# Attention's result kept as f32 until the MLPs, and two buffers for P^T and P's tail

## The chip, the cores and the metric

The kernel runs on one core of a Trainium2 chip. Its time is device microseconds (us) of one execution, as a median of the runs. TensorE (PE in the profile, PEld its weight loads), VectorE (DVE), ScalarE (ACT), GpSimd (POOL) and the DMA queue of SyncE (SP) work side by side, each on its own queue in program order, and wait for each other through semaphores. Attention's and the MLPs' operands lie in SBUF; TensorE writes only to PSUM, which has eight banks.

## The reference

Attention over 4 batches, 8 heads, 576 positions and 64 values per head, with rotated q and k, and then two MLPs over all 2304 tokens of width 512:

```python
q_rot, k_rot = rotate(q), rotate(k)
scores = scale * q_rot @ k_rot.T
attn = exp(scores - max(scores)); attn = attn / (sum(attn) + 1e-9)
x = (attn @ v).transpose(0, 2, 1, 3).reshape(2304, 512)
x = (1 / (1 + exp(-(x @ moe_w_gate))) * (x @ moe_w_val)) @ moe_w_out   # 512 -> 1536 -> 512
h = x @ moe2_w_in                                                      # 512 -> 2048
out = (h * (1 / (1 + exp(-1.702 * h)))) @ moe2_w_out                   # 2048 -> 512
```

All inputs and outputs are float32. (The weights arrive as 8-byte numbers and are decoded to float32 on the core.)

## The kernel before

**Number format.** A product in the MLPs is made of three passes: each operand is kept as a high part (rounded to the format fp32r) and a low part (value minus high part), and `split_mm` (L415) adds low weights x high activations, high weights x low activations, and high x high. For the activations these parts lie in the tiles `xhl[n]`: 128 partitions, 2 parts, 4 pieces of the model width, and the columns of block n. The 2304 tokens make five blocks, four of 512 and one of 256. The whole of `xhl` lies in the pool `big`, which lives for the whole kernel, with one buffer for each block.

**Attention** goes over 16 pairs of heads (4 batches x 4), and each pair over nine units, one for each 128 queries of a head, and one for the tails of 64 queries of both heads. A unit's scores (L295, L296) go to one of two PSUM buffers `pss`; DVE takes the row maximum `nm` (L298); ACT makes the exponentials (L313) into `P` (or `Pt` for the tails, one buffer); DVE makes reciprocals `r`, POOL scales P (L331). TensorE transposes P in pieces of 128 columns against the identity (L356; the tail in L363 with 64 columns as weights, and L368) into one of three PSUM banks `pt`, which ACT (L343) or DVE (L341) copies to the SBUF tiles `PT0` (first 256 queries) and `PT1` (other 320), one buffer each. The product P V (L386, two heads side by side in 64 columns of the array each; L383 for the tails of both) is summed over five steps in the one PSUM bank `ps_x`, first with PT0, then with PT1: two pieces per pair. When a piece is done, `split` in `pv` (L403) is put on a list `later` that the next slot works off: ACT copies the piece out of PSUM as the high part into `xhl` (L407), then DVE subtracts it from PSUM into the low part (L409). A piece that crosses the edge of a block makes two such steps, so that there are 24 steps of 256 columns and 24 shorter ones. The next piece's first P V must wait for both.

**The order of attention** is written out by hand. Slot G stands for unit G % 9 of pair G / 9; tables of lags (ROPE_MUL, PT, PV) say how many slots after its pair's first one each step comes. In a slot the steps follow the list in `slot` (L587): scores first, then rotation (`rope_mul`, `rope_add`, `transpose_qk`), one step of weight decoding, the list `later`, transposes of P, loads, P V, and the exponentials. The rotated q and k of the next pairs are transposed on TensorE (L234, into a bank `pt` too), split by ACT (L243) and DVE (L244), and moved to the layouts X, Y, Z, Zs by six transfers on SP's queue (L274). All 144 units' scores are issued by slot 143; the last pair's transposes and P V follow in the drain, slots 144 to 163. After it the pools `rot` (rotation's tiles, `pss`) and `soft` (P, PT, the other PSUM banks) are closed, and the MLPs' pools are opened in the space that comes free. A tile there waits only for the tiles that it overlaps.

**The MLPs** go over chunks of 256 hidden columns (6 and 8 of them) and in each over the five blocks. `hidden` (L439) makes 48 matmuls for a block in the first MLP, 24 in the second, with four PSUM buffers `psh`; ACT and DVE make the gated product and its parts. The output product of the block before follows (`out1`, `out2`: 24 matmuls), and DVE adds it to an f32 tile `acc[n]`, which lies in the MLPs' pool. At the last chunk of the first MLP `out1` makes new high and low parts of `acc` for the second (L482 on ACT, L483 on POOL). Between blocks the next chunk's weights are loaded and decoded (L133 to L139).

Of the kernel before, what the change touches and what calls it, by code (L numbers as in the profile page):

```python
# [8 lines left out]
F32 = mybir.dt.float32  # L9
F32R = mybir.dt.float32r  # L10
U32 = mybir.dt.uint32
AF = mybir.ActivationFunctionType
# [4 lines left out]
P = 128  # L17
# [9 lines left out]
def f(ap):  # L27
    return ap.bitcast(F32)
# [3 lines left out]
def attention_then_mlps(  # L32
# [32 lines left out]
    sp = soft.enter_context(tc.tile_pool(name="soft", bufs=1))  # L65
    stage_a = soft.enter_context(tc.tile_pool(name="stage_a", bufs=1))
    ps_t = soft.enter_context(tc.tile_pool(name="ps_t", bufs=1, space=PSUM))
    rp = rot.enter_context(tc.tile_pool(name="rope", bufs=1))
    ps_s = rot.enter_context(tc.tile_pool(name="ps_s", bufs=2, space=PSUM))

    cos_sb = rp.tile([P, NCHK, D], F32, name="cos_sb")
# [2 lines left out]
    vtail = [sp.tile([P, P], F32, tag=f"vtail{n}", name=f"vtail{n}") for n in range(2)]  # L74


    xhl = {}

    def new_xhl(n):
        xhl[n] = big.tile([P, 2, KT, width[n]], F32R, tag=f"xhl{width[n]}", name=f"xhl{n}", bufs=width.count(width[n]))  # L80


    stage = [stage_a]
# [217 lines left out]
    def exps(i, u):  # L301

        j, h = divmod(u, 2)
        ps = st[i].pop(("ps", u))
        nm = st[i]["nm"][:, h, j : j + 1]
        if h == 0:
            st[i]["P"][j] = (
                sp.tile([P, 2 * S], F32, tag="P", name="P", bufs=4)
                if j < MAINC
                else sp.tile([P, S], F32, tag="Pt", name="Pt", bufs=1)  # L310
            )
        c = h * S
        nc.scalar.activation(  # L313
            st[i]["P"][j][:, c : c + S].rearrange("p (n c) -> p n c", n=2),
            ps[:, :, :HALF],
            AF.Exp,
            bias=nm,
            accum_out=st[i]["sum"][:, u : u + 1],
        )
# [25 lines left out]
    def transpose_p(i, j, g):  # L345


        a = 0 if j < 2 else 1
        if (j, g) in ((0, 0), (2, 0)):
            st[i]["PT", a] = sp.tile([P, NCHK, PIECES[a][1]], F32, tag=f"PT{a}", name=f"PT{a}", bufs=1)  # L350
        PT = st[i]["PT", a]
        pt = st[i]["P"][j]
        ps = ps_t.tile([P, 512], F32, tag="pt", name="ps_p", bufs=3)
        if j < MAINC:
            for t in range(3):
                nc.tensor.transpose(  # L356
                    ps[:, t * P : (t + 1) * P], pt[:, (3 * g + t) * P : (3 * g + t + 1) * P], ident
                )
            jo = (j - 2 * a) * P
            dst = PT[:, 3 * g : 3 * g + 3, jo : jo + P]  # L360
            copy((j, g) in (PT_DVE if i else PT_DVE_FIRST), dst, ps[:, : 3 * P].rearrange("p (t c) -> p t c", t=3))
        elif g == 0:
            nc.tensor.transpose(ps[:TAIL, :P], pt[:, 0:TAIL], ident)  # L363
            for h in range(2):
                copy((j, g) in (PT_DVE if i else PT_DVE_FIRST), PT[h * TAIL : (h + 1) * TAIL, MAINC, 2 * P :], ps[:TAIL, h * TAIL : (h + 1) * TAIL])
        else:
            for t in range(MAINC):
                nc.tensor.transpose(ps[:, t * P : (t + 1) * P], pt[:, TAIL + t * P : TAIL + (t + 1) * P], ident)  # L368
            src = ps.rearrange("p (t h c) -> p h t c", t=MAINC, h=2)
            for h in range(2):  # L370
                t = h * (MAINC + 1)
                copy((j, g) in (PT_DVE if i else PT_DVE_FIRST), PT[:, t : t + MAINC, 2 * P :], src[:, h])

    def pv(i, a, ts):
        b, hp = divmod(i, NPAIR)
        PT, vt = st[i]["PT", a], st[i]["v"]
        c0, n = PIECES[a]
        if ts[0] == 0:
            st[i]["pv"] = ps_t.tile([P, 512], F32, tag="pv", name="ps_x", bufs=1)
        ps = st[i]["pv"]  # L380
        for t in ts:
            if t == MAINC:
                nc.tensor.matmul(ps[:, :n], st[i]["vtail"], PT[:, MAINC, :], start=False, stop=True)  # L383
                continue
            for h in range(2):
                nc.tensor.matmul(  # L386
                    ps[h * D : (h + 1) * D, :n],
                    vt[:, h * MAINC + t, :],
                    PT[:, h * (MAINC + 1) + t, :],
                    start=(t == 0),  # L390
                    stop=False,
                )
        if ts[-1] != MAINC:
            return
        parts = []
        g, c = b * S + c0, 0
        while c < n:
            blk, o = divmod(g + c, BLK)
            w = min(n - c, BLK - o)
            parts.append((blk, o, c, w))  # L400
            c += w

        def split():  # L403
            for blk, o, c, w in parts:
                if blk not in xhl:
                    new_xhl(blk)
                nc.scalar.activation(xhl[blk][:, 0, hp, o : o + w], ps[:, c : c + w], AF.Copy)  # L407
            for blk, o, c, w in parts:
                nc.vector.tensor_tensor(  # L409
                    xhl[blk][:, 1, hp, o : o + w], ps[:, c : c + w], f(xhl[blk][:, 0, hp, o : o + w]), ALU.subtract  # L410
                )

        later.append(split)

    def split_mm(ps, l, r, n):  # L415

        for sl, sr in ((1, 0), (0, 1), (0, 0)):
            for a in range(n):
                nc.tensor.matmul(  # L419
                    ps, l(sl, a), r(sr, a), start=(sl == 1 and a == 0), stop=(sl + sr == 0 and a == n - 1)  # L420
                )

    mlp = {}

    def hidden_m(kind, W, n, m, g):
        x, wd = xhl[n], width[n]
# [15 lines left out]
            hidden_m(kind, W, n, m, g)  # L442
        return g

    acc = {}
    row_runs = []
    for t in range(NT // P):
        runs = []
# [10 lines left out]
            c += n  # L459
        row_runs.append(runs)  # L460

    def new_acc(n):
        acc[n] = mlp["acc"].tile(
            [P, KT * width[n]], F32, tag=f"acc{width[n]}", name=f"acc{n}", bufs=width.count(width[n])
        )

    def out1(c, nchunk, W, n, g):
        if c == 0:
            new_acc(n)
        wd = width[n]  # L470
        if c == nchunk - 1:
            new_xhl(n)
        for e in range(KT):
            ps = mlp["ps_o"].tile([P, 512], F32, tag="pso", name="pso")
            split_mm(ps[:, :wd], lambda s, m: W.w_out(s, m, e * P, P), lambda s, m: g[:, s, m, :], MT)
            a = acc[n].rearrange("p (e w) -> p e w", w=wd)[:, e, :]
            if c == 0:
                nc.vector.tensor_copy(a, ps[:, :wd])
            else:
                nc.vector.tensor_tensor(a, ps[:, :wd], a, ALU.add)  # L480
            if c == nchunk - 1:
                nc.scalar.activation(xhl[n][:, 0, e, :], a, AF.Copy)  # L482
                nc.gpsimd.tensor_tensor(xhl[n][:, 1, e, :], a, f(xhl[n][:, 0, e, :]), ALU.subtract)  # L483

    def out2(c, nchunk, W, n, g):
        if c == 0:
            new_acc(n)
        for t in range(width[n] // P):
            ps = mlp["ps_o"].tile([P, 512], F32, tag="pso", name="pso")
            split_mm(ps[:, :DM], lambda s, m: g[:, s, m, t * P : (t + 1) * P], lambda s, m: W.w_out(s, m, 0, DM), MT)  # L490
            a = acc[n][:, t * DM : (t + 1) * DM]
            if c == 0:
                nc.vector.tensor_copy(a, ps[:, :DM])
            else:
                nc.vector.tensor_tensor(a, ps[:, :DM], a, ALU.add)  # L495
            if c == nchunk - 1:
                for x, (o, m, row, step) in enumerate(row_runs[n * BLK // P + t]):
                    (nc.gpsimd if x and n == NBLK - 1 else nc.sync).dma_start(out=out[row : row + (m - 1) * step + 1 : step, :], in_=a[o : o + m, :])
# [19 lines left out]

    DEC_PAIR, DEC_UNIT = (3, 4)
    FILL = 2  # L520
    dec = []

    def lags(table, i):
# [58 lines left out]
    def slot(G):  # L582
# [5 lines left out]
        for step in steps:  # L588
            step(G)

    with tc.manual_schedule():
        load(0)
        nc.gpsimd.dma_start(out=sin_sb, in_=sin_t)
# [12 lines left out]
        wts[1, 0] = Weights(1, 0)  # L606
        for G in range(-14, NU * npairs + 20):
            slot(G)
            i, u = divmod(G, NU)
            if DEC_PAIR <= i < DEC_PAIR + wts[1, 0].n:  # L610
                if u == 0:
                    wts[1, 0].load(i - DEC_PAIR)
                if u == DEC_UNIT:
                    dec += wts[1, 0].decode(i - DEC_PAIR)
        rot.close()
        soft.close()

        mlp["p"] = mlp["acc"] = ctx.enter_context(tc.tile_pool(name="mlp", bufs=1, reuse_waits="tile"))
        stage[0] = ctx.enter_context(tc.tile_pool(name="stage_m", bufs=2, reuse_waits="tile"))
        wpools[1] = mlp["p"]  # L620
        mlp["ps_o"] = ctx.enter_context(tc.tile_pool(name="ps_o", bufs=4, space=PSUM, reuse_waits="tile"))
# [2 lines left out]
        for at, (kind, c) in enumerate(chunks):  # L624
# [6 lines left out]
            done = 0  # L631
            for n in range(NBLK):
                W = wts[kind, c]
                g = hidden(kind, W, n)
                if pend is not None:
                    pend[0](*pend[1:])
                pend = (out1, c, FF1 // FFC, W, n, g) if kind == 1 else (out2, c, FF2 // FFC, W, n, g)
                for i in range(done, done + share[n]):
                    if i + 1 < wts[nxt].n:
                        wts[nxt].load(i + 1)  # L640
                    for op in wts[nxt].decode(i):
                        op()
                done += share[n]
# [56 lines left out]
```

## Time and profile before

| | |
|---|---|
| time, median of 3 runs (range) | 1158.08 us (1157.78 to 1158.6) |
| profiled execution: first to last instruction | 1156.3 us (of this execution the page has no other time) |
| TensorE busy, matmuls / weight loads | 97% / 80% |
| DVE, ACT, POOL busy | 65%, 37%, 28% |
| attention, one steady pair | about 18.0 us |
| MLPs | from 314.5 us to the end |

Times in the profile are us from the start of the span. "Busy" counts an engine's instructions only; matmuls overlap, and their ends are modelled. An idle time in brackets stands before the instruction, with the one that ended it by the semaphores; where several semaphores are waited for, that name can be wrong. "Issue" means a wait that the profile does not explain. A row with xN merges N like instructions that follow each other. A form such as 128\*64 gives the rows and columns of TensorE's weights.

### The profile page before, as it was taken

Reading aid. Unit: us, or ns where it says so; the run is one execution under the profiler, and the core shown is the slowest. Engines: PE = TensorE matmul, PEld = TensorE weight load, DVE = VectorE, ACT = ScalarE, POOL = GpSimd, SP = SyncE. Lnnn points to the kernel's source line nnn. Section 1 sums busy time; section 2 is a strip of 40 time slices with the busy share of each in tenths; the row PEclk is TensorE's granted clock in tenths of the full one; section 3 lists DMA queues with packets and bytes.
Section 4 is the critical chain, followed back from the end, with each engine's and each line's share of the span. In section 5 each row is a group of like instructions: output and inputs, shape, how many; then the busy total and the mean of one; then the engine's idle time right before and its main releaser. Section 6 shows DMA issues by size and latency. Waiting matters only on the chain.

```text
span 1156.3 us, 16339 instructions
## 1 busy us (share of the span) xinstructions
PE 1125.3 (97%) x6032; PEld 926.1 (80%) x6032; DVE 753.4 (65%) x1467; ACT 425.7 (37%) x937; POOL 324.3 (28%) x335
## 2 busy tenths in 40 slices
PE   3999999999999999999999999999999999999998
PEld 2777777777688888888888888888888888888886
DVE  6788897776454655545555455666767776676744
ACT  3777777777521211221212122342222223232221
POOL 6778787764210100100101002430010010010100
PEclk9999999999999999999999999999999999999999
DMA  4555665544110111111111111111111111111014
GB/s 133 138 145 150 144 165 131 118 100 99 39 53 20 54 38 37 55 37 37 55 37 55 37 37 37 34 39 39 38 46 45 37 55 37 37 55 37 19 37 128
DMA packets 46063, 76.15 MB, mean 66 GB/s; under 512 B 11728, under 2 KB 24016, under 8 KB 45984
## 3 DMA queue, kind: packets, MB, share of 16 engines
q1 hardware_dynamic: 45696, 74.19, 23.9%
q8 instruction: 48, 0.79, 0.3%
q0 software_dynamic: 288, 0.92, 0.2%
q14 instruction: 31, 0.25, 0.1%
HBM read 50.46 MB, written 4.72 MB: 48 GB/s over the span
## 4 chain that ended last, share of the span: by engine, by line
PE 83%; DVE 6%; DMA 5%; SPq 3%; issue 1%; ACT 1%; POOL 0%; POOLq 0%; DVEq 0%; ACTq 0%
PE psh L419 43%; PE pso L419 30%; PE ps_x L386 3%; PE ps_p L356 2%; PE pss L295 2%; DVE xr L219 2%; PE pss L296 2%; DMA Zs<-X 1%; DVE nm L298 1%; DMA X<-Y 1%; SPq L179 1%; DVE Y L244 1%; DVE PT L341 1%; PE ps_x L383 1%; DMA x<-in_k_dram 1%
## 5 line engine op out<-in xcount | busy, mean ns | idle before, releaser
L419 PE MATMUL psh<-xhl,w_in 128*128 128x512 f32 (+1 forms) x2400 | 504.3, 368 | 0.0
L419 PEld LDWEIGHTS psh<-xhl,w_in 128*128 128x128 f32 x2400 | 419.5, 189 | 75.7
L433 ACT ACTIVATE sg<-psh 128x512 f32<-128x512 f32 (+1 forms) x140 | 77.7, 555 | 366.9 <-PE psh L419 366.2
L419 PE MATMUL pso<-w_out,g 128*128 128x512 f32 x864 | 202.4, 389 | 0.0
L435 DVE TENSOR_TENSOR gf<-psh,sg 128x512 f32<-128x512 f32 (+1 forms) x140 | 89.1, 636 | 158.1 <-PE psh L419 111.6
L419 PEld LDWEIGHTS pso<-w_out,g 128*128 128x128 f32 x864 | 161.7, 188 | 33.2
L436 ACT ACTIVATE g<-gf 128x512 fp32r<-128x512 f32 (+1 forms) x140 | 82.5, 589 | 242.5 <-DVE gf L435 242.5
L139 POOL TENSOR_TENSOR w_in<-wt,w_in 128x512 fp32r<-128x512 f32 x40 | 51.8, 1294 | 391.0 <-DVE w_in L138 391.0
L437 DVE TENSOR_TENSOR g<-gf,g 128x512 fp32r<-128x512 f32 (+1 forms) x140 | 95.3, 681 | 91.7 <-ACT g L436 91.7
L419 PE MATMUL pso<-g,w_out 128*128 128x512 f32 (+1 forms) x720 | 152.8, 368 | 0.0
L419 PEld LDWEIGHTS pso<-g,w_out 128*128 128x128 f32 x720 | 125.8, 189 | 22.6
L298 DVE TENSOR_REDUCE nm<-pss 128x1 f32<-128x576 f32 x144 | 107.8, 749 | 52.3 <-PE pss L296 51.2
L331 POOL TENSOR_SCALAR P<-P,r 128x576 f32<-128x576 f32 x128 | 103.9, 824 | 73.2 <-DVE r L328 25.8
L139 POOL TENSOR_TENSOR w_out<-wt,w_out 128x512 fp32r<-128x512 f32 x28 | 36.2, 1293 | 263.9 <-DVE w_out L138 263.9
L313 ACT ACTIVATE P<-pss,nm 128x576 f32<-128x576 f32 x128 | 95.5, 746 | 32.5 <-DVE nm L298 31.8
L495 DVE TENSOR_TENSOR acc<-pso,acc 128x512 f32<-128x512 f32 x126 | 83.2, 686 | 20.3 <-PE pso L419 18.0
L386 PE MATMUL ps_x<-PT,v 128*64 128x320 f32 (+1 forms) x512 | 79.3, 420 | 4.2 <-DVE xhl L409 4.2
L356 PE MATMUL ps_p<-ident,P 128*128 128x128 f32 x576 | 81.7, 273 | 0.9 <-POOL P L331 0.9
L480 DVE TENSOR_TENSOR acc<-pso,acc 128x512 f32<-128x512 f32 (+1 forms) x100 | 61.6, 635 | 28.7 <-PE pso L419 28.7
L343 ACT ACTIVATE PT<-ps_p 128x384 f32<-128x384 f32 (+2 forms) x178 | 71.5, 440 | 21.9 <-PE ps_p L356 21.2
L356 PEld LDWEIGHTS ps_p<-ident,P 128*128 128x128 f32 x576 | 67.9, 140 | 2.2 <-POOL P L331 1.4
L295 PE MATMUL pss<-X 128*128 128x288 f32 (+3 forms) x176 | 54.6, 337 | 1.1 <-ACT P L313 0.5
(62 smaller groups left out, 1034.5 us busy)
## 6 DMA issues: line engine op xcount, KB each, us to landing
raw<-in_moe_w_out_dram SPq DMA_DIRECT2D x28, 512.0 KB, 3.5
raw<-in_moe_w_in_dram SPq DMA_DIRECT2D x16, 512.0 KB, 3.7
raw<-in_moe_w_gate_dram SPq DMA_DIRECT2D x12, 512.0 KB, 3.9
raw<-in_moe_w_val_dram SPq DMA_DIRECT2D x12, 512.0 KB, 3.8
Z<-X SPq DMA_DIRECT2D x15, 288.0 KB, 3.0
Z<-Y SPq DMA_DIRECT2D x15, 288.0 KB, 3.2
X<-Y SPq DMA_DIRECT2D x15, 288.0 KB, 3.1
x<-in_q_dram SPq DMA_DIRECT2D x16, 256.0 KB, 3.1
```

The source lines that it names most:

```text
L139: lambda: nc.gpsimd.tensor_tensor(w[:, 1, :], f(t), f(w[:, 0, :]), ALU.subtract),
L295: nc.tensor.matmul(ps[:m, n, o : o + w], T[:, q0 : q0 + m], rhs, start=True, stop=False)
L298: nc.vector.tensor_reduce(nm, ps[:, :, :HALF], axis=AX.XY, op=ALU.max, negate=True)
L313: nc.scalar.activation(st[i]["P"][j][:, c : c + S].rearrange("p (n c) -> p n c", n=2), ps[:, :, :HALF], AF.Exp, bias=nm, accum_out=st[i][" ...
L331: nc.gpsimd.tensor_scalar(pt, pt, r[:, c - a : c - a + 1], 1.0, op0=ALU.mult, op1=ALU.mult)
L356: nc.tensor.transpose(ps[:, t * P : (t + 1) * P], pt[:, (3 * g + t) * P : (3 * g + t + 1) * P], ident)
L386: nc.tensor.matmul(ps[h * D : (h + 1) * D, :n], vt[:, h * MAINC + t, :], PT[:, h * (MAINC + 1) + t, :], start=(t == 0), stop=False,)
L419: nc.tensor.matmul(ps, l(sl, a), r(sr, a), start=(sl == 1 and a == 0), stop=(sl + sr == 0 and a == n - 1))
L435: nc.vector.tensor_tensor(gf, pss[-1][:, :wd], sg, ALU.mult)
L436: nc.scalar.activation(g[:, 0, m, :], gf, AF.Copy)
L437: nc.vector.tensor_tensor(g[:, 1, m, :], gf, f(g[:, 0, m, :]), ALU.subtract)
L495: nc.vector.tensor_tensor(a, ps[:, :DM], a, ALU.add)
```

## The change

The three parts of the change are these. First, `split` in `pv` makes one f32 copy on ACT out of PSUM, into a tile `xf[blk]`; the high and low parts are made from it later by `split_block`, for each block four copies on ACT and four subtractions, on POOL and DVE in turn. Block 0 is split after slot 154, in the drain, into a pool opened in the space of the rotation's tiles; block n + 1 is split in the first chunk of the MLPs before `hidden` of block n. The MLPs' `acc[n]` now takes the buffers of `xf[n]`. Rotation's tiles and `xhl` lie at the right end of SBUF. Second, PT0, PT1 and Pt get two buffers. Third, the transpose of P's tail in L363 takes 128 columns instead of 64 (the copies after it take the same 64 as before).

```diff
-    rp = rot.enter_context(tc.tile_pool(name="rope", bufs=1))
+    rp = rot.enter_context(tc.tile_pool(name="rope", bufs=1, side="right"))
...
     def new_xhl(n):
-        xhl[n] = big.tile([P, 2, KT, width[n]], F32R, tag=f"xhl{width[n]}", name=f"xhl{n}", bufs=width.count(width[n]))
+        xhl[n] = mlp["x", min(n, 1)].tile([P, 2, KT, width[n]], F32R, tag=f"xhl{n}", name=f"xhl{n}", bufs=1)
+
+    def new_f32(n, name):
+        return big.tile(
+            [P, KT * width[n]], F32, tag=f"f32_{width[n]}", name=f"{name}{n}", bufs=width.count(width[n])
+        )
+
+    def split_x(n, e, src, eng):
+        a = src.rearrange("p (e w) -> p e w", w=width[n])[:, e, :]
+        nc.scalar.activation(xhl[n][:, 0, e, :], a, AF.Copy)
+        eng.tensor_tensor(xhl[n][:, 1, e, :], a, f(xhl[n][:, 0, e, :]), ALU.subtract)
...
-                else sp.tile([P, S], F32, tag="Pt", name="Pt", bufs=1)
+                else sp.tile([P, S], F32, tag="Pt", name="Pt", bufs=2)
...
-            st[i]["PT", a] = sp.tile([P, NCHK, PIECES[a][1]], F32, tag=f"PT{a}", name=f"PT{a}", bufs=1)
+            st[i]["PT", a] = sp.tile([P, NCHK, PIECES[a][1]], F32, tag=f"PT{a}", name=f"PT{a}", bufs=2)
...
-            nc.tensor.transpose(ps[:TAIL, :P], pt[:, 0:TAIL], ident)
+            nc.tensor.transpose(ps[:, :P], pt[:, 0:P], ident)
...
         def split():
             for blk, o, c, w in parts:
-                if blk not in xhl:
-                    new_xhl(blk)
-                nc.scalar.activation(xhl[blk][:, 0, hp, o : o + w], ps[:, c : c + w], AF.Copy)
-            for blk, o, c, w in parts:
-                nc.vector.tensor_tensor(
-                    xhl[blk][:, 1, hp, o : o + w], ps[:, c : c + w], f(xhl[blk][:, 0, hp, o : o + w]), ALU.subtract
-                )
+                if blk not in xf:
+                    xf[blk] = new_f32(blk, "xf")
+                at = hp * width[blk] + o
+                nc.scalar.activation(xf[blk][:, at : at + w], ps[:, c : c + w], AF.Copy)
...
-            new_acc(n)
+            acc[n] = new_f32(n, "acc")
...
+    def split_block(n):
+        new_xhl(n)
+        for e in range(KT):
+            split_x(n, e, xf[n], nc.vector if e % 2 else nc.gpsimd)
...
             slot(G)
+            if G == NU * npairs + DRAIN:          # DRAIN = 10
+                rot.close()
+                mlp["x", 0] = ctx.enter_context(tc.tile_pool(name="xhl_a", bufs=1, side="right", reuse_waits="tile"))
+                split_block(0)
...
-        rot.close()
         soft.close()
 
-        mlp["p"] = mlp["acc"] = ctx.enter_context(tc.tile_pool(name="mlp", bufs=1, reuse_waits="tile"))
+        mlp["x", 1] = ctx.enter_context(tc.tile_pool(name="xhl_b", bufs=1, side="right", reuse_waits="tile"))
+        mlp["p"] = ctx.enter_context(tc.tile_pool(name="mlp", bufs=1, reuse_waits="tile"))
...
                 W = wts[kind, c]
+                if at == 0 and n + 1 < NBLK:
+                    split_block(n + 1)
                 g = hidden(kind, W, n)
```

## Rows read from the trace of the kernel before

**Rows 1.** Busy us and instructions by stretch: a steady pair, the drain, the MLPs.

```profile
core 0: us, PE busy (x) PEld busy (x) DVE busy (x) ACT busy (x) POOL busy (x), PEclk, DMA share, GB/s
225.00:243.00 18.00, 17.62 (x131) 13.60 (x129) 13.58 (x38) 13.21 (x35) 12.94 (x16) 1.00 0.53 125
297.00:314.50 17.50, 16.57 (x114) 10.55 (x113) 7.22 (x21) 8.66 (x23) 4.70 (x7) 1.00 0.20 62
336.00:1150.00 814.00, 814.00 (x3885) 686.57 (x3884) 500.71 (x837) 199.85 (x353) 100.91 (x80) 1.00 0.14 43
```

**Rows 2.** Waits, whole span: engine, line, waited for; us, times, longest.

```profile
PEld ps_x L386 <- PE ps_p L356: 5.8, 12, 0.5
...
PE ps_x L386 <- DVE xhl L409: 4.2, 13, 0.9
...
PEld ps_p L363 <- issue: 3.8, 13, 0.3
```

**Rows 3.** Timeline of a steady pair: start us, duration, instruction, [idle before].

```profile
225.85 0.38 ACT L407 ACTIVATE xhl<-ps_x 128x256 fp32r<-128x256 f32 x1
...
226.21 0.87 ACT L343 ACTIVATE PT<-ps_p 128x384 f32<-128x384 f32 x2
...
226.68 0.38 PEld L356 LDWEIGHTS ps_p<-ident,P 128*128 128x128 f32 x3
...
227.04 0.41 DVE L409 TENSOR_TENSOR xhl<-ps_x,xhl 128x256 fp32r<-128x256 f32 x1
...
227.57 0.77 PEld L386 LDWEIGHTS ps_x<-PT,v 128*64 128x64 f32 x8 [0.51 <-PE ps_p L356]
```

**Rows 4.** Timeline, the same hand-over after the last rope work.

```profile
281.31 0.74 PEld L386 LDWEIGHTS ps_x<-PT,v 128*64 128x64 f32 x8 [0.16 <-issue]
```

**Rows 5.** Timeline of the steady pair: the last transfer of X and X's use.

```profile
229.53 0.49 SPq L274 DMA_DIRECT2D X<-Y  x1
...
233.26 0.19 PEld L295 LDWEIGHTS pss<-X 128*128 128x128 f32 x1
```

**Rows 6.** The page's DMA issues: count, size each, median us to landing.

```profile
X<-Y SPq DMA_DIRECT2D x15, 288.0 KB, 3.1
```

**Rows 7.** Timeline of the drain's end and the MLPs' first weights.

```profile
310.47 0.38 ACT L407 ACTIVATE xhl<-ps_x 128x256 fp32r<-128x256 f32 x1 [1.63 <-PE ps_x L383]
...
311.37 1.81 PEld L386 LDWEIGHTS ps_x<-PT,v 128*64 128x64 f32 x16 [1.33 <-DVE xhl L409]
...
314.05 2.06 PEld L419 LDWEIGHTS psh<-xhl,w_in 128*128 128x128 f32 x9
```

**Rows 8.** Groups by line and shape: busy us, mean ns, idle before.

```profile
L356 PEld LDWEIGHTS ps_p<-ident,P 128*128 128x128 f32 x576 | 67.9, 140 | 2.2 <-POOL P L331 1.4 <-ACT PT L343 0.2
```

**Rows 9.** Timeline around the tail's transpose in the steady pair.

```profile
239.02 0.56 DVE L244 TENSOR_TENSOR Y<-ps_qk,X 128x384 fp32r<-128x384 f32 x1
...
239.69 0.11 PEld L363 LDWEIGHTS ps_p<-ident,Pt 128*64 128x64 f32 x1 [0.29 <-issue]
...
239.92 0.20 PEld L386 LDWEIGHTS ps_x<-PT,v 128*64 128x64 f32 x4
```

**Rows 10.** Groups by line and shape: the MLPs' splits of 512 columns.

```profile
L437 DVE TENSOR_TENSOR g<-gf,g 128x512 fp32r<-128x512 f32 x112 | 77.7, 694 | 78.2 <-ACT g L436 78.2
...
L483 POOL TENSOR_TENSOR xhl<-acc,xhl 128x512 fp32r<-128x512 f32 x16 | 20.2, 1297 | 26.7 <-ACT xhl L482 26.7
...
L482 ACT ACTIVATE xhl<-acc 128x512 fp32r<-128x512 f32 x16 | 10.1, 632 | 10.3 <-DVE acc L480 10.3
```

**Rows 11.** Chain of waits: start us, us, what; a block's 48 matmuls.

```profile
341.69 10.88 PE psh L419 x48
```

**Rows 12.** Timeline, weight decoding in the MLPs' first chunk.

```profile
330.49 1.33 POOL L139 TENSOR_TENSOR w_in<-wt,w_in 128x512 fp32r<-128x512 f32 x1 [24.71 <-DVE w_in L138]
330.71 1.39 DVE L135 TENSOR_SCALAR wt<-wc 128x512 uint32<-128x512 uint32 x1
```

**Rows 13.** Timeline near the kernel's start: a weight load after idle time.

```profile
22.45 0.34 PEld L295 LDWEIGHTS pss<-Z 128*128 128x128 f32 x1
```

More of the change, by code (lines that the diff above doesn't have):

```diff
@@ L74, in attention_then_mlps @@
     vtail = [sp.tile([P, P], F32, tag=f"vtail{n}", name=f"vtail{n}") for n in range(2)]
+    mlp = {}
     xhl = {}
+    xf = {}
+    acc = {}
     def new_xhl(n):
-        xhl[n] = big.tile([P, 2, KT, width[n]], F32R, tag=f"xhl{width[n]}", name=f"xhl{n}", bufs=width.count(width[n]))
+        xhl[n] = mlp["x", min(n, 1)].tile([P, 2, KT, width[n]], F32R, tag=f"xhl{n}", name=f"xhl{n}", bufs=1)
[7 more added lines that the diff above has]
+        eng.tensor_tensor(xhl[n][:, 1, e, :], a, f(xhl[n][:, 0, e, :]), ALU.subtract)
     stage = [stage_a]
@@ L421, in split_mm @@
                 )
-    mlp = {}
     def hidden_m(kind, W, n, m, g):
@@ L443, in hidden @@
         return g
-    acc = {}
     row_runs = []
@@ L460, in attention_then_mlps @@
         row_runs.append(runs)
[L462 to L465, printed above, removed]
     def out1(c, nchunk, W, n, g):
         if c == 0:
-            new_acc(n)
+            acc[n] = new_f32(n, "acc")
         wd = width[n]
@@ L481, in out1 @@
             if c == nchunk - 1:
-                nc.scalar.activation(xhl[n][:, 0, e, :], a, AF.Copy)
-                nc.gpsimd.tensor_tensor(xhl[n][:, 1, e, :], a, f(xhl[n][:, 0, e, :]), ALU.subtract)
+                split_x(n, e, acc[n], nc.gpsimd)
     def out2(c, nchunk, W, n, g):
         if c == 0:
-            new_acc(n)
+            acc[n] = new_f32(n, "acc")
         for t in range(width[n] // P):
@@ L520, in attention_then_mlps @@
     FILL = 2
+    DRAIN = 10
     dec = []
```

## The prediction

> **What bounds the kernel now.** I read the page first, then the busy time by stage, then who waits on TensorE (PE and its weight loads PEld), then one steady attention pair instruction by instruction. The page's part 1 shows TensorE busy nearly throughout; the stages show two regimes [rows 1]: in the MLPs PE has no idle time at all (814.00 of 814.00 us), in a steady attention pair 17.62 of 18.00 us, and in the drain of the last pair 16.57 of 17.50. So work on ACT, DVE and POOL costs nothing by itself; time can only come from waits that stand in TensorE's queue. The waits view names one wait for the code that the change touches [rows 2]: PE's P V matmul (L386) on DVE's low-part subtraction (L409), 4.2 us in 13 places, and at the same places PEld's 5.8 us in 12 places (put down to ps_p, which had long been done). A pair and both ends of attention then show what stands there.
>
> **The L409 wait, pair by pair.** There is one PSUM bank ps_x for P V. At the end of a piece ACT makes the high part (L407), DVE the low part (L409), and both must be done before the next piece's first weights load. In a steady pair [rows 3] ACT is done at 225.85 + 0.38 = 226.23; DVE, behind its copies, starts L409 only at 227.04 and ends at 227.45; L386's weights load at 227.57, 0.12 us later, after 0.51 us idle. In the pair after the last rope work DVE comes sooner, and L386 starts with 0.16 us idle [rows 4]: that is the floor of this hand-over, whoever frees the bank. The change makes L407 the bank's only reader. What is late next? PEld's own floor: the three loads before end at 227.06, + 0.16 = 227.22. And P^T's last ACT copy, which this product needs: 226.21 + 0.87 = 227.08, + 0.12 = 227.20. Both allow a start 0.35 us sooner, so nothing takes most of the gain back. Per place 5.8/12 - 0.16 = 0.32 us; 12 places: **-3.9 us**. Ends: nothing (ACT's copy comes later than in these rows) to 12 x 0.35 = -4.2.
>
> Does a shorter pair run into something else? The next pair's X comes by a chain of transfers; the last one is issued at 229.53 [rows 5] and lands some 3.1 us later [rows 6], at 232.6, for weights loaded at 233.26. With PE 0.32 us earlier 0.3 us of room is left. Tight, but enough.
>
> **The last pair.** L386 of the second piece loads at 311.37, after 1.33 us idle, because L407 (310.47 + 0.38 = 310.85) is followed by L409 [rows 7]. Freed by L407 it starts at 310.85 + 0.12 = 310.97: **-0.4 us** (ends: 0 to -0.4).
>
> **The 128-wide transpose of P's tail (L363).** Its weights grow from 64 to 128 columns. A load of 128 columns in a transpose takes 140 ns [rows 8], this one 0.11 us [rows 9]: 0.03 us more in each of 16 pairs, **+0.5 us**. It idles 0.29 us in 13 pairs [rows 2]; in the pair of rows 9 DVE's L244, which frees the PSUM bank that L363 takes (third one back), ends at 239.02 + 0.56 = 239.58, and L363 loads 0.11 us later. The change does not touch that, so I leave it. Ends: that wait gone for another reason, -3.8; or a change of weight width that costs the 0.16 us floor once more in each pair, 16 x 0.16 = +2.6. In rows 9 the L386 after it follows at 0.23 us, with none of the 0.16 us idle. The Trainium skill, "TensorEngine Tiling (Array Packing)", section "Key Properties", says that switching the tiling mode drains the engine; by it the switch would only move from before L363 to after it, and the sum would keep about these 0.1 us a pair either way. Rows 9 can't tell that drain from the bank wait.
>
> **Two buffers for P^T and P's tail.** They save a wait only where a copy waits for an older P V. In rows 3 the P^T copies start as L407 ends, without idle, and none of the places in rows 2 is of that kind. **0** (ends: 0 to -0.4, the size of a place).
>
> **What moves to the MLPs.** DVE loses 48 subtractions, none of which holds PE but at the places above. New are 20 high-part copies on ACT and 20 subtractions, half on DVE, half on POOL: by their nearest rows 0.63, 0.69 and 1.30 us for 512 columns [rows 10]. Blocks 1 to 4 are split one block ahead: 4 x 0.63 = 2.5 us on ACT in front of the block's first sigmoid, within 10.9 us of matmuls (48 at 0.227 each [rows 11]), whose outputs have four PSUM buffers; weight decoding and the sigmoids queue behind, and PE, busy without a gap there, reaches their results many us later. Cost 0; without that cover up to 2.5 us once per block. The weights for the second chunk may load later than now, since they now lie over attention's own tiles; they are needed only about 70 us on.
>
> Block 0 is different: it is split in the drain, and PE needs it at once. ACT gets to it after L407, at 310.85: high parts at 311.5, 312.1, 312.75, 313.4. PE's first MLP weights load at 314.05 now [rows 7], at 313.65 then. The first four matmuls take high parts, and the low ones are wanted from 314.56 to 315.24. POOL and DVE read both inputs from SBUF. In the MLPs a DVE operation that met POOL's subtraction took 1.39 us instead of 0.43 and ended as POOL did [rows 12]; so I let the four run one after another: 311.6 + 1.3 + 0.7 + 1.3 + 0.7 = 315.6, **+0.35 us**. Run side by side they end at 314.2 and cost 0; if PE waits for the whole of block 0 before its first matmul, 315.7 - 313.65 = 2.0. The Trainium skill, "SBUF — State Buffer", section "Who interferes with whom", calls the port pair that DVE shares with GpSimd an exclusive lock, taken also by a DVE instruction with two SBUF inputs. The trace agrees in the 1.39 us; the sum with or without it differs by those 0.35 us.
>
> **Sum.** -3.9 - 0.4 + 0.5 + 0.35 = -3.45 us. The profiled execution has a span of 1156.3, so 1152.85 after. The runs' median is 1158.08, 1.8 above the span, taken as the same: **1154.6 us**, 0.3% faster. The ends added up (whole-block wait, without the rival below) are 1149.3 and 1162.7.
>
> **Rivals.**
> 1. *The wait is replaced by half of itself.* With L409 gone, L386 waits for ACT's second P^T copy, or the next pair for X. For it: both lie within 0.35 us [rows 3, 5]. Against: with 0.16 us idle in rows 4 neither shows. Gain 12 x 0.16 = 1.9: 1158.08 - 1.9 - 0.4 + 0.85 = 1156.6.
> 2. *Slower: the MLPs start starved.* Block 0's parts lie where the rope tiles were. If their storage, or the queues that make them, come free only as PE reaches the MLPs (313.65 by the new count), the high parts start at 313.77, the four serial subtractions end 0.63 + 0.12 + 4.0 us later, and PE starts at 318.6: 5.0 us late. Near the kernel's start, after idle time, a 128-column load took 0.34 us [rows 13] instead of the 0.19 of rows 5, though the granted clock reads full there; if PE's next 12 matmuls (2.7 us) ran at that pace, they would lose 2.7 x (0.34/0.19 - 1) = 2.1. 7.1 - 3.8 = +3.3: 1161.4. It cancels the gain from a loss of 3.8 us and is visibly slower from 6.1. Against: the rope tiles' readers end before the drain, at the last scores.
> 3. *DVE's relief reaches L363 too.* 13 x 0.29 = 3.8 more: 1150.8. Against: L244 ends as late as before, as it waits for ACT.
> 4. *It does nothing:* another reader keeps the bank as late. 1158.08 + 0.85 = 1158.9.
>
> **How the numbers follow.** Chances: forecast 58%, rival 1 20%, rival 2 9%, rival 3 6%, rival 4 7%. About 0.2% (2.3 us) is what a measurement here can tell from no change: faster means under 1155.8, slower over 1160.4. The forecast is faster but for an eighth of its chance (whole-block wait, dearer L363); rival 1 falls nearly all in between. Faster 0.51 + 0.06 + 0.05 = 62%, same 28%, slower (rival 2 and a little of 4) 10%. Range 1152.4 to 1158.5: it leaves out rivals 2 and 3 and part of 4.
>
> **What would show it.** After: the wait of L386 on DVE is gone from the waits view; L386's place has 0.16 to 0.2 us idle; a steady pair takes 17.7 us instead of 18.03; the first MLP load comes 3.5 to 4 us sooner, and PE idles less than half a us among the first 12 MLP matmuls; the MLPs keep their length. Wrong would be a new wait of L386 on ACT's P^T copy, of scores on the transfer of X, L363's neighbours idling more, or PE idle for us at the MLPs' start.

## The result and the profile after

The changed kernel takes 1172.65 us (median of 4 runs, 1171.61 to 1173.35) against 1158.23 for the kernel before: a ratio of 1.0123, interval 1.0108 to 1.0137. It is 14.4 us slower. 1154.6 was forecast, with a range to 1158.5: the sign was wrong. The profiled execution's span grew from 1156.3 to 1170.9 us.

Read the stages first. The end of attention is where the MLPs' first weights load: 314.05 before [rows 7], 313.20 after, in this timeline of the changed kernel's drain (start us, duration, instruction, idle before; L399 and L421 are the old L386 and L407, L92 and L93 are the new splits, L429 is the old L419):

```profile
310.08 0.38 ACT L421 ACTIVATE xf<-ps_x 128x256 f32<-128x256 f32 x1 [1.63 <-PE ps_x L396]
310.38 2.19 ACT L92 ACTIVATE xhl<-xf 128x512 fp32r<-128x512 f32 x4
310.52 1.81 PEld L399 LDWEIGHTS ps_x<-PT,v 128*64 128x64 f32 x16 [0.88 <-ACT xf L421]
...
311.09 2.96 POOL L93 TENSOR_TENSOR xhl<-xf,xhl 128x512 fp32r<-128x512 f32 x2 [6.49 <-ACT xhl L92]
311.56 3.04 DVE L93 TENSOR_TENSOR xhl<-xf,xhl 128x512 fp32r<-128x512 f32 x2 [3.97 <-ACT xhl L92]
...
313.20 3.27 PEld L429 LDWEIGHTS psh<-xhl,w_in 128*128 128x128 f32 x14
```

So the MLPs begin 0.85 us sooner, where 3.5 to 4 us were forecast, and everything from there to the end went from 1156.3 - 314.05 = 842.25 to 1170.9 - 313.20 = 857.7 us: the MLPs lost 15.45. PE doesn't start late there (no idle before its first load) and doesn't wait later. In the windows view the stretch of [rows 1] in the middle of the MLPs is still full, at the full granted clock, but it holds 3809 matmuls instead of 3885:

```profile
336.00:1150.00 814.00, 814.00 (x3809) 674.09 (x3808) 500.50 (x828) 202.20 (x358) 108.25 (x86) 1.00 0.13 41
```

An engine that is busy but slower shows in the duration of its instructions and in their count, not in its busy share. The groups by line and shape of the kernel before (first fence) and of the changed one (second fence; busy us, mean ns, idle before):

```profile
L419 PE MATMUL psh<-xhl,w_in 128*128 128x512 f32 x1920 | 444.5, 389 | 0.0
L419 PE MATMUL pso<-w_out,g 128*128 128x512 f32 x864 | 202.4, 389 | 0.0
L419 PE MATMUL pso<-g,w_out 128*128 128x512 f32 x576 | 134.6, 389 | 0.0
```

```profile
L429 PE MATMUL psh<-xhl,w_in 128*128 128x512 f32 x1920 | 457.8, 396 | 0.0
...
L429 PE MATMUL pso<-w_out,g 128*128 128x512 f32 x864 | 203.7, 391 | 0.0
...
L429 PE MATMUL pso<-g,w_out 128*128 128x512 f32 x576 | 135.4, 390 | 0.0
...
L429 PE MATMUL psh<-xhl,w_in 128*128 128x256 f32 x480 | 59.9, 282 | 0.0
```

The 512-column products that read xhl lose 13.3 us, the two pso forms 1.3 and 0.8: 15.4 together, all of the loss. The 256-column products that read xhl keep their time (59.8 us before). The chain shows it is no single event but a steady pace, 11.21 us for 48 matmuls where [rows 11] has 10.88 (0.2335 us each instead of 0.2267; 1920 x 0.0069 = 13.2):

```profile
336.05 5.48 PE pso L429 x24
341.53 11.21 PE psh L429 x48
352.74 5.48 PE pso L429 x24
```

In attention the forecast holds in part. L399 in two steady pairs late in attention (first fence) and in two pairs that also decode a piece of the first weights (second fence), both from the timeline of weight loads:

```profile
227.84 0.74 PEld L399 LDWEIGHTS ps_x<-PT,v 128*64 128x64 f32 x8 [0.17 <-ACT PT L356]
...
245.52 0.74 PEld L399 LDWEIGHTS ps_x<-PT,v 128*64 128x64 f32 x8 [0.17 <-ACT PT L356]
```

```profile
101.55 0.19 PEld L399 LDWEIGHTS ps_x<-PT,v 128*64 128x64 f32 x2 [0.17 <-ACT PT L356]
101.89 0.73 PEld L399 LDWEIGHTS ps_x<-PT,v 128*64 128x64 f32 x6 [0.15 <-ACT PT L356]
...
119.58 0.19 PEld L399 LDWEIGHTS ps_x<-PT,v 128*64 128x64 f32 x2 [0.17 <-ACT PT L356]
```

The idle time fell from 0.51 [rows 3] to 0.17, and a pair takes 17.68 us instead of 18.03. But in the six decoding pairs the period stays 18.03: the eight products begin after 0.17, do two, and wait again for a copy of P^T. ACT's queue there points at the reason (e9 tests it): its decoding operation stands ahead of L421 and of both copies:

```profile
100.14 0.68 ACT L146 ACTIVATE wc<-raw 128x512 f32<-128x512 f32 x1
...
100.72 0.36 ACT L421 ACTIVATE xf<-ps_x 128x256 f32<-128x256 f32 x1
...
100.99 0.85 ACT L356 ACTIVATE PT<-ps_p 128x384 f32<-128x384 f32 x2
```

### The profile page after: what moved, and what is told of

The parts are those of the page before. It is cut to its first block, busy times and chain, and to the rows that moved or that the text cites. A ratio compares the mean times of both kernels' runs of the same rounds, so it can differ in the third digit from the quotient of the medians.

```text
span 1170.9 us, 16297 instructions
## 1 busy us (share of the span) xinstructions
PE 1143.1 (98%) x6032; PEld 927.5 (79%) x6032; DVE 763.0 (65%) x1429; ACT 435.1 (37%) x957; POOL 338.4 (29%) x345
## 3 DMA queue, kind: packets, MB, share of 16 engines
HBM read 50.46 MB, written 4.72 MB: 47 GB/s over the span
## 4 chain that ended last, share of the span: by engine, by line
PE 95%; DMA 1%; DVE 1%; issue 1%; ACT 1%; SPq 1%; POOL 0%; POOLq 0%; DVEq 0%; ACTq 0%
PE psh L429 43%; PE pso L429 29%; PE ps_x L399 6%; PE ps_p L369 5%; PE pss L308 4%; PE pss L309 3%; PE ps_x L396 2%; PE ps_qk L247 1%; DMA x<-in_k_dram 1%; PE ps_p L381 1%; DMA Zs<-X 0%; DVE nm L311 0%; DVE xr L232 0%; ACT P L326 0%; PE ps_p L376 0%
## 5 line engine op out<-in xcount | busy, mean ns | idle before, releaser
L429 PE MATMUL psh<-xhl,w_in 128*128 128x512 f32 (+1 forms) x2400 | 517.7, 373 | 0.0
L429 PEld LDWEIGHTS psh<-xhl,w_in 128*128 128x128 f32 x2400 | 419.8, 188 | 87.9
L429 PE MATMUL pso<-w_out,g 128*128 128x512 f32 x864 | 203.7, 391 | 0.0
L429 PEld LDWEIGHTS pso<-w_out,g 128*128 128x128 f32 x864 | 161.6, 188 | 35.1
L429 PE MATMUL pso<-g,w_out 128*128 128x512 f32 (+1 forms) x720 | 153.5, 369 | 0.0
L429 PEld LDWEIGHTS pso<-g,w_out 128*128 128x128 f32 x720 | 125.7, 188 | 23.7
L399 PE MATMUL ps_x<-PT,v 128*64 128x320 f32 (+1 forms) x512 | 81.4, 421 | 0.5 <-ACT xf L421 0.5
```

Source lines behind the costliest of these rows:

```text
L399: nc.tensor.matmul(ps[h * D : (h + 1) * D, :n], vt[:, h * MAINC + t, :], PT[:, h * (MAINC + 1) + t, :], start=(t == 0), stop=False,)
L429: nc.tensor.matmul(ps, l(sl, a), r(sr, a), start=(sl == 1 and a == 0), stop=(sl + sr == 0 and a == n - 1))
```

## The experiments

The matmuls, their order and their data are unchanged in the MLPs; what differs is where xhl lies. In the compiled programs' memory maps (byte within a partition, modulo 2048; rows inside a tile are multiples of 512 bytes, so the remainder modulo 256 holds for every matmul of a tile):

```
                  w_in, w_out, g      xhl
before            128                 128, all five
after             128                 2016, all five (right end of SBUF: 229344)
```

Two theories came first: A, the moving operand (xhl) must start on a 64-byte boundary (2016 is 32 past one); B, the right end of SBUF is slow. Four kernels tell them apart.

**e1_right_aligned**: the changed kernel, xhl 32 bytes further left.

```diff
     big = ctx.enter_context(tc.tile_pool(name="big", bufs=1))
+    pad = ctx.enter_context(tc.tile_pool(name="pad", bufs=1, side="right"))
+    pad.tile([P, 8], F32, name="pad")
```

> The changed kernel with one 32-byte tile put first at the right end of SBUF, so that the rope tiles and xhl start at multiples of 64 bytes and no longer 32 bytes past one. Theory A (alignment): TensorE's reading of the moving operand is slower where its rows start 32 bytes off a 64-byte grid; the 48 psh matmuls of a 512-column block go back from 11.21 to 10.88 us, the MLPs lose their 15.4 us, and the time is about 1157 (1172.65 - 15.4). Rival B (place): xhl lies in another part of SBUF, apart from the weights, and that is slower; 11.2 us per block and about 1172.5 as before.

Measured 1163.24 us, ratio 1.0041 (1.0028 to 1.0055): between the two kernels, as neither theory has it. The chain's 48 take 11.00 us.

**e2_before_xhl_32**: the kernel before, each xhl tile 32 bytes later. The longer tiles also move what lies behind them.

```diff
-        xhl[n] = big.tile([P, 2, KT, width[n]], F32R, ...)
+        size, o = 2 * KT * width[n], (8, 8, 8, 8, 8)[n]
+        t = big.tile([P, size + 32], F32R, ...)
+        xhl[n] = t[:, o : o + size].rearrange("p (s k w) -> p s k w", s=2, k=KT)
```

> The kernel before, with nothing changed but that each xhl tile starts 32 bytes past a multiple of 64 (it stays in its old place, next to the weights). Theory A: 11.2 us instead of 10.88 for the 48 psh matmuls of a 512-column block, the 256-column block unchanged at 5.75, time 1158.2 + 15 = about 1173. Rival B: 10.88 and 1158.

Measured 1175.87, ratio 1.0149 (1.0136 to 1.0163), psh at 11.19 to 11.25. B falls: the loss comes without the right end. Here w_out and g are out of step too in every second chunk, where 24 pso matmuls take 5.57 to 5.60 us instead of 5.44.

**e3_before_stagger**: the same with offsets of 0, 16, 32, 64 and 32 bytes for blocks 0 to 4.

```diff
-        size, o = 2 * KT * width[n], (8, 8, 8, 8, 8)[n]
+        size, o = 2 * KT * width[n], (0, 4, 8, 16, 8)[n]
```

> The kernel before with xhl of blocks 0, 1, 2, 3, 4 shifted by 0, 16, 32, 64, 32 bytes from a multiple of 64. Theory A with a 64-byte grid: blocks 1 and 2 take 11.2 us for 48 psh matmuls, blocks 0 and 3 10.88. With a 32-byte grid: block 1 alone slow (and then the changed kernel's 32 bytes would not be the cause). Rival B: all 10.88.

Measured 1171.8 in one run.

**e4_before_weights_32**: the kernel before with the code of xhl left as it was and w_in and w_out of every second chunk, beginning with the first, 32 bytes later.

```diff
+        def shifted(self, name, size):
+            o = 8 if self.pool is big else 0
+            t = self.pool.tile([P, 2 * size + 32], F32R, tag=name, name=name, bufs=1)
+            return t[:, o : o + 2 * size].rearrange("p (s n) -> p s n", s=2)
...
-                self.w = self.pool.tile([P, 2, 2 * KT * FFC], F32R, tag="w_in", name="w_in", bufs=1)
+                self.w = self.shifted("w_in", 2 * KT * FFC)
...
-                self.o = self.pool.tile([P, 2, MT * DM], F32R, tag="w_out", name="w_out", bufs=1)
+                self.o = self.shifted("w_out", MT * DM)
```

> The kernel before with the weights of every second chunk (those in the first pool) starting 32 bytes past a multiple of 64. They are TensorE's stationary operand in psh and in the first MLP's pso, its moving operand in the second MLP's pso. Theory A, moving operand alone: psh unchanged (10.88 per block, 5.44 in the second MLP), the first MLP's pso unchanged at 5.44, the second MLP's pso in every second chunk 5.6 instead of 5.44 per 24; time +3 us or so (4 chunks x 18 x 0.16 / ... at most 4 x 4.5 x 0.16 = 2.9). If the stationary operand minds too, psh of every second chunk is slower as well. Rival B: nothing changes.

Measured 1173.08 in one run: 15 us lost although blocks 0 to 3 of xhl start at 128 as before. So A falls too: by it psh keeps 10.88. The next lines are from its chain. The first two psh rows belong to the chunk whose w_in starts at 160, the last two to the next chunk, whose w_in starts at 384:

```profile
342.41 11.20 PE psh L424 x48
353.61 5.60 PE pso L424 x24
359.21 11.20 PE psh L424 x48
...
387.29 10.91 PE psh L424 x48
398.20 2.87 PE pso L424 x24
401.07 10.91 PE psh L424 x48
```

xhl is the same, the weights differ: 160 - 128 = 32 is slow, 384 - 128 = 256 is not. And in e3 the blocks differ in one chunk (w_in at 768; blocks 0 to 3 in order, with xhl at 128, 528, 416, 320; by A the first and the last take 10.88):

```profile
387.13 11.14 PE psh L421 x48
...
401.15 11.12 PE psh L421 x48
...
417.76 11.24 PE psh L421 x48
...
434.48 11.00 PE psh L421 x48
```

Theory C: the pace depends on the difference of the two starts, weights less moving operand, modulo 256 bytes. The starts in the memory maps of e1 to e4, modulo 2048 (w_in: the two places that the chunks take in turn; xhl: blocks 0 to 3):

```
      w_in        xhl
e1    128, 128    1984, all
e2    640, 768    160, 544, 416, 288
e3    640, 768    128, 528, 416, 320
e4    160, 384    128, all
```

Collected from the chains of the kernel before, the changed one and e1 to e4, us per 48 psh matmuls of 512 columns:

```
difference   0            32     64     96           112    128    160          192    224          240
us           10.88-10.91  11.20  11.20  11.23-11.25  11.20  11.14  11.19-11.21  11.00  11.19-11.20  11.12
```

The pso products follow C too: 24 of 512 columns take 5.57 to 5.61 us where w_out and g are 128 or 160 apart (e2, e3, e4). The next two kernels were expected from C alone. **e5_in_phase**: e1 with another size of the dead tile; xhl is at 128, with all else as in the change.

```diff
-    pad.tile([P, 8], F32, name="pad")
+    pad.tile([P, 472], F32, name="pad")
```

> The changed kernel with a dead tile of 1888 bytes per partition first at the right end, so that every xhl tile starts at 128 modulo 2048 bytes, as w_in, w_out and g do (in the changed kernel it is 2016 for xhl, in the kernel before 128 for all). Theory C (what costs is the start of the weights less the start of the moving operand, modulo 256 bytes; a multiple of 256 is free): the chain's 48 psh matmuls of 512 columns take 10.88 us again, the MLPs 842 us from their first load, and with the attention's gain of 0.85 the time is 1157 to 1158 (ratio 0.999 to 1.000). Theory A (the moving operand's start off a 64-byte boundary) says the same here. Rival B (the right end of SBUF itself is slow): 11.0 or more, 1163 as in e1_right_aligned.

**e6_before_all_32**: the kernel before with everything moved together.

```diff
     big = ctx.enter_context(tc.tile_pool(name="big", bufs=1))
+    big.tile([P, 8], F32, name="pad")
```

> The kernel before with one dead tile of 32 bytes per partition ahead of all others, so that xhl, w_in, w_out and g all start at 160 modulo 2048: off every 64-byte boundary, but with a difference of 0 between weights and moving operand. Theory C: psh 10.88 to 10.9 per 48, the time that of the kernel before, 1158 (ratio 0.999 to 1.001, MLPs 842). Theory A: psh 11.2, pso 5.6, the time 1172 to 1178. The attention's tiles also move to 32 modulo 64; if that is what made the changed kernel's start 0.8 us longer, the first attention stage is 0.8 longer here too.

e5: 1156.67, ratio 0.9985 (0.9976 to 0.9994). e6: 1158.70, ratio 1.0003 (0.9994 to 1.0012). The groups of e5, and below them those of e6:

```profile
L431 PE MATMUL psh<-xhl,w_in 128*128 128x512 f32 x1920 | 444.6, 389 | 0.0
...
L431 PE MATMUL pso<-w_out,g 128*128 128x512 f32 x864 | 202.4, 389 | 0.0
...
L431 PE MATMUL pso<-g,w_out 128*128 128x512 f32 x576 | 134.6, 389 | 0.0
```

```profile
L420 PE MATMUL psh<-xhl,w_in 128*128 128x512 f32 x1920 | 444.6, 389 | 0.0
```

Both groups have the 444.5 us of the kernel before to a tenth: at the right end with the change, and 32 bytes off every 64-byte boundary. One dead tile takes 16 us out of the changed kernel. C holds; A would have put e6 at 1172 to 1178. In e5 the pso rows are back too. From their first load to the end the MLPs take 842.23 us in e5 and 842.21 to 842.29 in e7 to e11, which have the same addresses, against 842.25 in the kernel before: in step, the splits and all else that moved to the MLPs cost nothing.

With that repaired, what does the change itself bring? e5 lies a little under the 1157 to 1158 expected of it and gains 1.6 us of the 3.45 forecast. Five kernels look for the rest.

**e7_in_phase_copy_first**: e5, with the copies of ps_x ahead of the decoding step.

```diff
-            steps = (step_scores, step_rope, step_decode, run_later, step_pt, ...)
+            steps = (step_scores, step_rope, run_later, step_decode, step_pt, ...)
```

> As e5_in_phase, with the deferred copies of ps_x (run_later) issued ahead of the decoding step in each slot, so that ACT's decoding operation no longer stands before the copy of ps_x in the six pairs that decode weights. Theory (the six decoding pairs keep their old period of 18.03 because ACT's copy of ps_x comes behind the decoding operation): these six pairs shrink to 17.7, 6 x 0.34 = 2 us less than e5_in_phase, some 1155 to 1156. Rival (something else in these pairs, DVE's five decoding operations or the weights' DMA, sets 18.03): same as e5_in_phase within 0.4.

Measured 1156.16, ratio 0.9980 (0.9971 to 0.9989). The decoding pairs went only from 18.03 to 17.97: a miss, 0.5 us gained for 2 expected; ACT's decoding operation still stood ahead of the P^T copies.

**e8_in_phase_single_pt**: e5 without the buffers and the wider transpose.

```diff
-                else sp.tile([P, S], F32, tag="Pt", name="Pt", bufs=2)
+                else sp.tile([P, S], F32, tag="Pt", name="Pt", bufs=1)
...
-            st[i]["PT", a] = sp.tile([P, NCHK, PIECES[a][1]], F32, tag=f"PT{a}", name=f"PT{a}", bufs=2)
+            st[i]["PT", a] = sp.tile([P, NCHK, PIECES[a][1]], F32, tag=f"PT{a}", name=f"PT{a}", bufs=1)
...
-            nc.tensor.transpose(ps[:, :P], pt[:, 0:P], ident)
+            nc.tensor.transpose(ps[:TAIL, :P], pt[:, 0:TAIL], ident)
```

> As e5_in_phase, with one buffer again for PT0, PT1 and Pt, and the 64-column transpose of P's tail as before: what is left is the f32 result and the splits at the MLPs. Theory (double buffers and the 128-column transpose cost and give nothing that matters): as e5_in_phase within 0.7 us. Rival (the double buffers carry the attention's gain): the steady period is back at 18.03, 12 x 0.34 = 4 us more than where it is 17.69, and about 2 us more over the pairs that gained.

Measured 1155.82, ratio 0.9977 (0.9968 to 0.9986): 0.85 below e5, a little outside the 0.7 expected, on the fast side. The f32 result carries the whole gain, and the steady period is 17.64:

```profile
226.24 0.74 PEld L401 LDWEIGHTS ps_x<-PT,v 128*64 128x64 f32 x8 [0.17 <-ACT PT L358]
...
243.88 0.74 PEld L401 LDWEIGHTS ps_x<-PT,v 128*64 128x64 f32 x8 [0.17 <-ACT PT L358]
```

**e9_single_pt_decode_late**: e8, with the decoding step at the end of its slot and one unit later, where ACT has a gap.

```diff
-            steps = (step_scores, step_rope, step_decode, run_later, step_pt, ..., step_pv, step_exps)
+            steps = (step_scores, step_rope, run_later, step_pt, ..., step_pv, step_exps, step_decode)
...
-    DEC_PAIR, DEC_UNIT = (3, 4)
+    DEC_PAIR, DEC_UNIT = (3, 5)
```

> As e8_in_phase_single_pt, with the decoding step issued one slot later and at the end of its slot, so that ACT's decoding operation stands behind the exponential of unit 6, where ACT is idle for 0.6 us in the steady pairs, and no longer ahead of the copies of P^T in unit 5. Theory (in e7_in_phase_copy_first the decoding operation still stood ahead of those P^T copies, and they then end 0.3 late, in the middle of the 8 matmuls of PV): the six decoding pairs fall from 18.03 to 17.65, 6 x 0.38 = 2.3 us, 1153.5 in all. Rival (the weights' DMA or the engines' general load sets 18.0 there): same as e8_in_phase_single_pt within 0.4.

Measured 1154.48, ratio 0.9966 (0.9954 to 0.9979): the lowest median here, 1.3 us under e8 where 2.3 were expected. The first fence has the weight loads of a decoding pair in e8, the second those of two decoding pairs in e9; the second wait inside the eight products is gone:

```profile
100.80 0.19 PEld L401 LDWEIGHTS ps_x<-PT,v 128*64 128x64 f32 x2 [0.17 <-ACT PT L358]
101.21 0.73 PEld L401 LDWEIGHTS ps_x<-PT,v 128*64 128x64 f32 x6 [0.22 <-ACT PT L358]
```

```profile
118.92 0.74 PEld L401 LDWEIGHTS ps_x<-PT,v 128*64 128x64 f32 x8 [0.17 <-ACT PT L358]
...
136.69 0.73 PEld L401 LDWEIGHTS ps_x<-PT,v 128*64 128x64 f32 x8 [0.17 <-ACT PT L358]
```

A decoding pair takes 17.77 (136.69 - 118.92) instead of 18.03, except one that is 0.8 longer (there the last transfer, X<-Y, lands 4.72 us after its issue, and the scores on X load after 1.02 us idle): -0.26 each instead of the -0.38 expected. So the place of the decoding operation makes up two thirds of what these pairs lacked; the other 0.13 stays open.

**e10_single_pt_128_wide** and **e11_in_phase_64_wide**: e8 with the wide transpose alone, and with the double buffers alone (the lines of e8's diff, undone one by one).

> As e8_in_phase_single_pt, with the 128-column transpose of P's tail of the change and single buffers. Theory: 0.04 us in each of 16 pairs (period 17.69 against 17.65), 0.6 us more than e8_in_phase_single_pt, no stalls on late X; some 1156.4. Rival: the 0.9 us between e5_in_phase and e8_in_phase_single_pt is all from the double buffers, and this is e8_in_phase_single_pt within 0.2.

> As e8_in_phase_single_pt, with two buffers for PT0, PT1 and Pt (64-column transpose as before). Theory that the double buffers do nothing: e8_in_phase_single_pt within 0.2. Rival: they let the pair run so that a transfer into X is late in some pairs (in e5_in_phase Zs<-X took 5.0 us instead of 3.3 in two pairs, which were 0.65 longer): 0.5 to 1 us more than e8_in_phase_single_pt, with a wider spread.

e10: 1157.17, ratio 0.9989 (0.9980 to 0.9998). e11: 1156.36, ratio 0.9982 (0.9973 to 0.9991). The intervals of e8, e10 and e11 overlap. Run by run, all eleven of e10 (from 1156.36) lie above all ten of e8 (to 1156.07), measured in another round, in which the kernel before is 0.2 us longer: e10 missed the 1156.4 expected, and its "no stalls". The direct cost of the wide transpose is small: a load in it takes 140 ns in e10 and 108 in e8, and a pair without a stall 17.67 to 17.70 (228.30 to 246.00, the same rows) against 17.64. What parts the times further, by the profiles, is a stall that some pairs have in most of the shortened kernels: X's transfers end late. In e5's chain:

```profile
224.99 5.00 DMA Zs<-X
...
230.07 2.97 DMA X<-Y
233.04 0.14 issue
233.17 0.37 PE pss L310
```

Zs<-X takes 5.00 us where the page's median is 3.3, and the pair is 0.65 longer. e5's profile has two such pairs, the changed kernel, e7 and e11 one each, e10 three, e8 none. It comes with single buffers (e10) and with the 64-column transpose (e11), so neither the buffers nor the width is needed for it. But the runs of e8, which has neither, lie within 0.65 us, those of e5, e10 and e11 within 2.0 to 2.3: the wider spread of e11's rival came true, while its 0.5 us (1156.36 against 1155.82) are inside the overlap of the intervals. Why the transfer is longer in some pairs is open.

## Why the prediction was wrong, step by step

**The step that failed: "the MLPs keep their length".** Of the 18 us between forecast and result, 15.4 are this. Under "What moves to the MLPs" the prediction priced the new instructions, their queues and when storage comes free, and set blocks 1 to 4 at 0. It didn't price that the moved tiles get another address. The right-hand pools put xhl at 2016 instead of 128 modulo 2048, 160 bytes out of step with w_in, and 15.4 us went on 512-column matmuls that no wait, no idle time and no clock shows. All of it comes back with the addresses at the right end (e5), with nothing else in the MLPs changed; none of it comes with an equal shift (e6). What the prediction did price there was right: the MLPs of e5 take 842.23 us. The rivals had only ways of PE waiting; a slower PE was not among them. How the two addresses act on the pace is not shown. The weight loads themselves are no longer, here before and after; their engine idles more:

```profile
L419 PEld LDWEIGHTS psh<-xhl,w_in 128*128 128x128 f32 x2400 | 419.5, 189 | 75.7
...
L429 PEld LDWEIGHTS psh<-xhl,w_in 128*128 128x128 f32 x2400 | 419.8, 188 | 87.9
```

That a load and the reads of the matmul beside it get in each other's way when out of step is a guess: no run here took the loads away, and it doesn't say why 192 bytes cost less than the other differences.

**The L409 wait (-3.9).** The wait is gone, the idle time is 0.17 as said (0.16 to 0.2), and a steady pair takes 17.68. The count was wrong: 12 places were taken as alike from one steady pair, while six of them decode weights, and there rival 1's wait on ACT's P^T copy took its place whole. The rows of one decoding pair of the kernel before would have shown it:

```profile
99.74 0.68 ACT L133 ACTIVATE wc<-raw 128x512 f32<-128x512 f32 x1
...
100.57 0.88 ACT L343 ACTIVATE PT<-ps_p 128x384 f32<-128x384 f32 x2
...
100.93 0.41 DVE L409 TENSOR_TENSOR xhl<-ps_x,xhl 128x256 fp32r<-128x256 f32 x1
...
101.46 0.78 PEld L386 LDWEIGHTS ps_x<-PT,v 128*64 128x64 f32 x8 [0.44 <-PE ps_p L356]
```

L409 ends at 101.34 and ACT's second copy at 101.45: with the first gone, the second holds the product as long. The six places are 6 x 0.32 = 1.9 us, and -3.45 + 1.9 = -1.55 is near what e5's median has (-1.6). That fit is in part luck: block 0's +0.35 was not paid, and late transfers into X cost about 1.3 us in e5's profiled execution, whose span is 0.8 us under that of the kernel before (both terms below).

**X's room (0.3 us).** Called tight but enough. It is enough in most pairs and not in those where Zs<-X takes 5.0: the other half of rival 1, 0.65 to 0.75 us at a time.

**The last pair (-0.4).** L399 loads at 310.52, 0.06 us after L421's end (310.08 + 0.38), with 0.88 us idle instead of 1.33 [rows 7]: -0.45, right.

**The wide transpose (+0.5).** Right in its direct cost: 140 - 108 = 0.03 us more for the load (e10 and e8), 0.03 to 0.06 in a pair without a stall, 0.5 to 1 us in 16 pairs. The idle time before it stayed, as said (3.7 us in 13 places, 3.8 before). That e10 is 1.3 us over e8 was not in the sum.

**The two buffers (0).** They gain nothing, as said: e8 without them is the faster. Whether they cost the 0.5 us between e11 and e8 the runs can't tell.

**Block 0 (+0.35).** The serial running was nearly right: the four subtractions take 3.5 us, from 311.09 to 314.60, where 4.0 were reckoned one after another and 2.6 side by side. The groups of the changed kernel:

```profile
L93 POOL TENSOR_TENSOR xhl<-xf,xhl 128x512 fp32r<-128x512 f32 x8 | 11.9, 1515 | 7.2 <-ACT xhl L92 7.2
...
L93 DVE TENSOR_TENSOR xhl<-xf,xhl 128x512 fp32r<-128x512 f32 x8 | 10.9, 1400 | 4.6 <-ACT xhl L92 4.6
```

1400 ns instead of DVE's 694, 1515 instead of POOL's 1297 [rows 10]. That a DVE instruction with two SBUF inputs and a GpSimd instruction that reads SBUF hold each other up is what the Trainium skill says in "SBUF — State Buffer", section "Who interferes with whom"; these rows agree. (In [rows 12] the DVE operation has one SBUF input, and it ends 0.28 us after POOL's, not with it.) But it cost PE nothing: ACT began the high parts at 310.38 instead of 310.85, the low ones are done at 311.56 + 3.04 = 314.6, a us before the 315.6 reckoned, and PE's row at 313.20 runs on without idle. Rival 2 (a starved start) didn't happen.

**The start of attention.** The first P V weights load at 36.32 before and 37.09 after, 0.8 us that the prediction has no term for. Over the profiles here it lies between 36.25 and 36.99 where the attention is that of the kernel before, and between 36.21 and 37.09 where it is changed; so the 0.8 us does not come with the change. With one profile of each kernel, whether it is spread between executions or goes with the tiles' places is not shown (e6, which was to tell, has 36.99).

## What to carry to other kernels

When a change moves a tile that TensorE reads, look at its address beside that of the other operand, before and after; here a dead tile of 1888 bytes mended it. A loss without idle time is found in the mean duration of one instruction and in the count of a full window. A wait priced in one place is multiplied only over places with the same queues: look at one of each kind. When a stage gets shorter, the transfer with the least room becomes a stall in some rounds before it does in all.

## What the hardware showed that was not expected

- 48 back-to-back matmuls of 512 columns, each with its own 128-column weight load, take 10.88 to 10.91 us when weights and moving operand start at the same byte modulo 256, 11.00 at 192 bytes apart, 11.12 to 11.25 at the other differences tried (e1 to e6 and both kernels): up to 3.4%, with PE busy throughout and the clock at 1.00.
- The 256-column block gains nothing from being in step: 48 take 5.74 to 5.75 us in step and 5.60 to 5.76 out of step.
- The 24 pso matmuls take 5.48 instead of 5.44 in the changed kernel although w_out and g are in step there. They came back with xhl (e5); by what path is open.
